# S4D convolution beside a gated unit: preparation queued behind the gated unit's newest VectorE operation, in turns

## The chip, the cores and the metric

The kernel runs on one core of a Trainium2 chip. The metric is the device time of one execution in microseconds (us); of several runs the median is given. The engines are called by the profile's names: PE (TensorE matmuls), PEld (its weight loads), DVE (VectorE), ACT (ScalarE), POOL (GpSimd), SP (SyncE, which here only issues transfers).

## What is computed

One block of a model for 2048 tokens of 448 channels. It adds three terms: the input itself, a long convolution of the normalised input, and a gated unit on the same normalised input.

```python
def ssm(u, log_A_real, A_imag, C_real, C_imag, log_dt, D_skip):
    dt = jnp.exp(log_dt)
    A = -jnp.exp(log_A_real) + 1j * A_imag
    C = (C_real + 1j * C_imag) * dt[:, None]
    P = jnp.exp((A * dt[:, None])[:, :, None] * pos[None, None, :])
    K = 2.0 * jnp.einsum("dn,dnl->dl", C, P).real
    y = jnp.fft.irfft(jnp.fft.rfft(u_t, L2) * jnp.fft.rfft(K, L2), L2)[:, :, :L]
    return y_t + u * D_skip
def glu(x, w_gate, w_up, w_down):
    return (sigmoid(x @ w_gate) * (x @ w_up)) @ w_down
xn = layernorm(A_u)
return A_u + ssm(xn, ...) + glu(xn, ...)
```

Here L is 2048, L2 4096, `u_t` is `u` with channels ahead of tokens, there are 448 channels with 256 states each, and the gated unit has 1792 hidden features.

## The kernel before

**Two streams of work.** The program is written as two generators, `conv()` (L1017) and `glu()` (L727). A loop at the end (L1115) draws from the one whose finished share is smaller; each `yield` gives the planned cost of the work just traced, and the totals stand in L1111. The result is a traced order. From it a scheduler, with a timing estimate of its own, lays down the queue of each engine when the program is built; on the chip each queue runs in that order. Two things bend the order: `hp(HP)` raises the priority of what it encloses, and `tc.issue_after(ins)` keeps the enclosed instructions behind `ins` in the queue of `ins`'s engine. It puts nothing in front of anything.

**The convolution stream.** It normalises the first eight blocks of 128 tokens in two quarters of four and transposes them (`x_transpose`, L191), for the gated unit's first half. It then runs the preparation `prep` (L342), twice, for two halves of the channels (`h` 0 and 1): an exponential by polynomial (`exp`, L300), reciprocals in four pieces (`pieces`, L319), arctangent, sine and hyperbolic tangent on ACT, and phases `U`, `V`, `T` that are split into a high and a low part and stored to memory (L390 to L417). Its `yield`s cut it into portions. Two results, `pl` and `a3`, are turned by TensorE (`turn`, L429, transposes in L436) into the tables `W1` and `GG`. Between portions stand four first stages of the input's transform (`x_spec`, L280). Kernel generation (`kgen`, L458) follows in 56 chunks: POOL forms magnitudes from powers of `W1` (L452), ACT sines of the phases, DVE the products `Et` and `Ft` (L600 to L602), TensorE their sums `ko` (L614). The transforms in `spectra` (L839) come last.

**The gated unit.** It takes the tokens in two halves of 1024, and the 14 feature tiles in groups of three, the last of two. For a feature tile `f` and 512 tokens `t` (here called a unit), `gate` (L693) makes two products of 11 matmuls each (L706), since operands are kept as a high and a low part. ACT forms `th` (L714), DVE `hf` (L717), ACT its high part `hh` (L722), DVE the low part `hl` (L724). At the end of a group come eight products `po` (L817), each added by DVE to `acc` (L822). Weights are loaded by SP (L640, L642) into one buffer, and split by ACT (`wh`, L757) and DVE (`wl`, L761). Gate products, `po` and some others share four PSUM banks (`gu`).

**What orders the work around the change.** All portions of `prep`, and the statistics of the other eight blocks (`x_stats`, L245, L246, and `x_scales`, L248), compete with the gated unit for DVE. The statistics are traced in one piece ahead of the portions, behind the last operation of `x_transpose` (`xls`, L1071). Then, in rounds, one portion of each half is traced behind the third newest `hf` (`hfs`, `LAG`, L1086); a round is planned at 11/3. Transposes of `turn` stay behind the newest gate matmul traced (`glu_mm`, L433). In the traced order the last portion with DVE work lies between the two units of f4, and kernel generation beside the first unit of f5.

In `x_transpose` a quarter has four column blocks. Blocks 0 and 1 lie in one PSUM tile, `tr`, blocks 2 and 3 in tiles of their own, `ko` and `kp`:

```python
two = psc[-1].tile([128, 2, 512], F32, name="tr", bufs=1)
banks = [two[:, 0], two[:, 1]] + [psc[-1].tile([128, 512], F32, name=n, bufs=1) for n in ("ko", "kp")]
```

Each block is transposed (L209), copied by ACT (L218, L221) and subtracted by DVE (L219, L222) before the next block is traced.

Of the kernel before, what the change touches and what calls it, by code (L numbers as in the profile page):

```python
# [11 lines left out]
F32 = mybir.dt.float32  # L12
F32R = mybir.dt.float32r
# [20 lines left out]
WP = 11 / 3  # L34
# [14 lines left out]
LAG = 3  # L49
# [79 lines left out]
def s4d_glu_kernel(ctx, tc, io):  # L129
# [61 lines left out]
    def x_transpose(src, xs, o0):  # L191

        xh, xl, xr = xs
        nb = len(src)
        o = slice(o0, o0 + 128 * nb)

        if nb == 4:
            two = psc[-1].tile([128, 2, 512], F32, name="tr", bufs=1)
            banks = [two[:, 0], two[:, 1]] + [psc[-1].tile([128, 512], F32, name=n, bufs=1) for n in ("ko", "kp")]
        for k in range(4):  # L200
            kp = 128 if k < 3 else 64
            at = k * nb % 4
            if nb == 4:
                ps = banks[k]
            elif at == 0:
                ps = psg.tile([128, 512], F32, name="gu", bufs=4)
            for b in range(nb):
                c = 128 * (at + b)
                nc.tensor.transpose(ps[:kp, c : c + 128], src[b][:, 128 * k : 128 * k + kp], ident)  # L209
            p = ps[:kp, 128 * at : 128 * (at + nb)]  # L210
            if k == 0 and nb == 2:
                continue
            if k == 1 and nb == 2:
                p = ps.rearrange("p (k t) -> p k t", k=2)
                nc.scalar.copy(xh[:, 0:2, o], p)
                v.tensor_tensor(xl[:, 0:2, o], p, xh[:, 0:2, o], ALU.subtract)
            elif k < 3:
                nc.scalar.copy(xh[:, k, o], p)  # L218
                v.tensor_tensor(xl[:, k, o], p, xh[:, k, o], ALU.subtract)  # L219
            else:  # L220
                mv = nc.scalar.copy(xr[0:64, o], p)  # L221
                xls[:] = [v.tensor_tensor(xr[64:128, o], p, xr[0:64, o], ALU.subtract)]  # L222
                act[:] = [mv]

# [468 lines left out]
    def gate(w, xs, to, between=None):  # L693
# [24 lines left out]
        hfs.append(marks[1])  # L718
# [4 lines left out]
        with hp(HP):  # L723
            v.tensor_tensor(hl, hf, hh, ALU.subtract)  # L724
        to.append((hh, hl))

    def glu():  # L727
        stores = []
        for half in range(2):
# [4 lines left out]
            for fs_ in ORDER[half]:  # L734
# [70 lines left out]
                for t in range(2):  # L805
                    acc = accs[2 * half + t]
                    for b in range(4):
# [13 lines left out]
                        with hp(HP):  # L821
                            v.scalar_tensor_tensor(  # L822
                                acc[:, b], po, 0.5, acc[:, b], ALU.mult, ALU.add
                            )
# [192 lines left out]
    def conv():  # L1017
        with tc.tile_pool(name="psk", bufs=1, space=PSUM) as ps_, tc.tile_pool(
# [9 lines left out]
            with tc.tile_pool(name="pst", bufs=1, side="right", reuse_waits="tile") as pst:  # L1028
# [42 lines left out]
                with tc.issue_after(xls[0].ins):  # L1071
                    for b in range(8):
                        x_stats(sm, 8 + b, xes[b // 4][:, b % 4])
                x_scales(sm, 8, 8)

                p01 = pst.tile([CP, 2, 2, 2 * N], F32R, name="p01", tag="xe0")
                for i in range(2):
                    slots[f"P{i}"] = p01[:, i]
                x1ab = pst.tile([128, 2, 2, D], F32, name="x1ab", tag="xe1")
                slots["x1a"], slots["x1b"] = x1ab[:, 0], x1ab[:, 1]  # L1080

                n = 0
# [24 lines left out]
    lasts, glu_mm, sp_mm, glu_on, outs, x1s, hfs, xls = [], [], [], [], [0], [0], [], []  # L1107
# [3 lines left out]
    total = [sum(Y0) + 15 * WP + 8 * WX + 14 + NCK * WK + HOLE + 17 * WS, 2 * (4 + NFT * 14.8) - HELD]  # L1111
# [41 lines left out]
```

## Time and profile before

| | |
|---|---|
| median of 3 runs | 738.23 us (736.59 to 740.59) |
| profiled execution | 739.08 us |
| its span in the trace | 737.3 us |
| TensorE busy | 677.7 us |
| VectorE busy | 565.4 us |

A row of the timeline has the start in the span, the duration (of several in a row, from the first's start to the last's end), engine, line, operation, output and inputs, shapes and count; in brackets the engine's idle time ahead of it and what ended it. Rows of one engine can overlap by some tens of ns, since operations are pipelined. SPq is SP's queue issuing a transfer.

### The profile page before, as it was taken

Reading aid. Unit: us, or ns where it says so; the run is one execution under the profiler, and the core shown is the slowest. Engines: PE = TensorE matmul, PEld = TensorE weight load, DVE = VectorE, ACT = ScalarE, POOL = GpSimd, SP = SyncE. Lnnn points to the kernel's source line nnn. Section 1 sums busy time; section 2 is a strip of 40 time slices with the busy share of each in tenths; the row PEclk is TensorE's granted clock in tenths of the full one; section 3 lists DMA queues with packets and bytes.
Section 4 is the critical chain, followed back from the end, with each engine's and each line's share of the span. In section 5 each row is a group of like instructions: output and inputs, shape, how many; then the busy total and the mean of one; then the engine's idle time right before and its main releaser. Section 6 shows DMA issues by size and latency. Waiting matters only on the chain.

```text
span 737.3 us, 19085 instructions
## 1 busy us (share of the span) xinstructions
PE 677.7 (92%) x7780; PEld 533.9 (72%) x7780; DVE 565.4 (77%) x776; ACT 421.6 (57%) x654; POOL 369.8 (50%) x423
## 2 busy tenths in 40 slices
PE   2896799999998979989999999999999999998994
PEld 2674687887876768655678887888877787775783
DVE  5799997899999888998468969977956555554553
ACT  3534656669679667998467778776643312313310
POOL 2101064987987937865535875877844003241001
PEclk9988999999999999999999999999999999999998
DMA  9935385344413454354953242232269999999756
GB/s 208 227 88 162 80 257 183 99 141 138 157 51 105 155 175 135 109 185 113 289 151 118 76 151 86 77 108 75 75 169 262 261 248 238 230 240 232 182 138 163
DMA packets 93287, 116.76 MB, mean 158 GB/s; under 512 B 12176, under 2 KB 81168, under 8 KB 92944
## 3 DMA queue, kind: packets, MB, share of 16 engines
q1 hardware_dynamic: 83888, 95.08, 47.6%
q10 hardware_dynamic: 6736, 14.57, 6.4%
q0 software_dynamic: 2576, 5.90, 3.4%
q8 instruction: 61, 1.00, 0.6%
q14 instruction: 26, 0.21, 0.1%
HBM read 70.75 MB, written 44.76 MB: 157 GB/s over the span
## 4 chain that ended last, share of the span: by engine, by line
PE 57%; DVE 17%; DMA 9%; POOL 7%; issue 4%; ACT 3%; SPq 3%; ACTq 0%; DVEq 0%; POOLq 0%
PE gu L706 20%; PE po L817 16%; PE sp L899 5%; PE ko L614 5%; PE pv L926 3%; PE tr L538 3%; POOL mf L516 3%; POOL me L516 2%; DVE Ft L602 2%; DVE Et L601 2%; DVE Et L600 1%; DMA sx<-x_d 1%; DMA tb<-in_c_tab_dram 1%; DVE pm L452 1%; PE kp L564 1%
## 5 line engine op out<-in xcount | busy, mean ns | idle before, releaser
L516 POOL TENSOR_TENSOR me<-me,pm 128x32 f32<-128x32 f32 (+1 forms) x168 | 137.0, 815 | 94.0 <-DVE Et L601 85.0
L516 POOL TENSOR_TENSOR mf<-mf,pm 128x64 f32<-128x64 f32 (+1 forms) x112 | 127.2, 1135 | 4.7
L706 PE MATMUL gu<-xh,wh 128*128 128x512 f32 x336 | 102.1, 411 | 3.7 <-ACT xh L218 3.7
L706 PE MATMUL gu<-xh,wl 128*128 128x512 f32 x336 | 96.4, 394 | 0.0
L706 PE MATMUL gu<-xl,wh 128*128 128x512 f32 x336 | 96.2, 391 | 0.0
L817 PE MATMUL po<-dh,hh 128*128 128x448 f32 x224 | 85.5, 382 | 11.3 <-DVE hf L717 7.3
L602 DVE TENSOR_TENSOR Ft<-mf,S 128x1024 f32<-128x1024 f32 x56 | 79.1, 1413 | 17.0 <-PE ko L614 9.3
L601 DVE TENSOR_TENSOR Et<-me,S 128x1024 f32<-128x1024 f32 x56 | 77.9, 1391 | 9.9 <-ACT me L529 8.4
L600 DVE TENSOR_TENSOR Et<-me,S 128x1024 f32<-128x1024 f32 x56 | 80.4, 1438 | 5.8 <-ACT S L549 5.0
L817 PE MATMUL po<-dl,hh 128*128 128x448 f32 x224 | 83.5, 373 | 0.0
L817 PE MATMUL po<-dh,hl 128*128 128x448 f32 x224 | 82.7, 372 | 0.0
L546 ACT ACTIVATE S<-tr 128x1024 f32<-128x1024 f32 x56 | 57.7, 1030 | 42.8 <-PE tr L538 38.5
L614 PEld LDWEIGHTS ko<-Et,Ft 128*32 128x32 f32 x3584 | 54.5, 111 | 35.6 <-DVE Ft L602 15.0
L706 PEld LDWEIGHTS gu<-xh,wh 128*128 128x128 f32 x336 | 62.6, 194 | 23.0 <-ACT xh L218 5.2
L614 PE MATMUL ko<-Et,Ft 128*32 128x64 f32 x3584 | 65.5, 222 | 13.6 <-DVE Ft L602 12.6
L722 ACT CAST hh<-hf 128x512 fp32r<-128x512 f32 x56 | 34.9, 622 | 71.8 <-DVE hf L717 56.3
L706 PEld LDWEIGHTS gu<-xh,wl 128*128 128x128 f32 x336 | 64.1, 191 | 14.8 <-issue 0.7
L706 PEld LDWEIGHTS gu<-xl,wh 128*128 128x128 f32 x336 | 63.1, 188 | 14.1 <-issue 0.7
L822 DVE SCALAR_TENSOR_TENSOR acc<-po,acc 128x448 f32<-128x448 f32 x80 | 48.5, 616 | 22.6 <-PE po L817 22.4
L717 DVE SCALAR_TENSOR_TENSOR hf<-th,gu 128x512 f32<-128x512 f32 x56 | 38.2, 682 | 35.8 <-PE gu L706 31.3
L549 ACT ACTIVATE S<-S,hpi 128x1024 f32<-128x1024 f32 x56 | 65.5, 1169 | 0.0
L714 ACT ACTIVATE th<-gu 128x512 f32<-128x512 f32 x56 | 33.7, 602 | 47.8 <-PE gu L706 47.6
(204 smaller groups left out, 1306.0 us busy)
## 6 DMA issues: line engine op xcount, KB each, us to landing
sk_d<-sk ACTq DMA_DIRECT2D x14, 512.0 KB
sx<-x_d SPq DMA_DIRECT2D x32, 224.0 KB
skl<-sk_d SPq DMA_DIRECT2D x16, 448.0 KB
vp<-v_d SPq DMA_DIRECT2D x16, 448.0 KB
v_d<-vt SPq DMA_DIRECT2D x62, 112.0 KB
wt_d<-wh SPq DMA_DIRECT2D x9, 512.0 KB
wt_d<-wl SPq DMA_DIRECT2D x9, 512.0 KB
wl<-wt_d SPq DMA_DIRECT2D x9, 512.0 KB
```

What stands on the lines that cost most here:

```text
L516: ins = nc.gpsimd.tensor_tensor(m[:, :, w + a : 2 * w : n], m[:, :, a:w:n], par(base + i).unsqueeze(2).to_broadcast([128, 4 * DC, w // n]) ...
L546: nc.scalar.activation(rows(cs), pv, AF.Abs)
L549: sins[:] = [nc.scalar.activation(cs, cs, AF.Sin, scale=-TWO_PI, bias=hpi)]
L600: v.tensor_tensor(Et[:, :, :, 32:64], two(me[:, :, 32:64]), S[:, 1::-1], ALU.mult)
L601: v.tensor_tensor(Et[:, :, :, 0:32], two(me[:, :, 0:32]), S[:, 1:3, :, ::-1], ALU.mult)
L602: fts[:] = [v.tensor_tensor(Ft, two(mf), S[:, 3:5], ALU.mult)]
L614: mm = nc.tensor.matmul(ko[32 * j : 32 * j + 32, sl], Ft[:, cc, DC * h + 4 * q + j], Et[:, cc, DC * h + 4 * q + j], start=(k == 0), stop=( ...
L706: glu_mm[:] = [nc.tensor.matmul(ps, a_, b_, start=(n == 0), stop=(n == len(mm) - 1))]
L717: marks[1] = v.scalar_tensor_tensor(hf, th, 1.0, pgu[1], ALU.add, ALU.mult)
L817: glu_mm[:] = [nc.tensor.matmul(po, a_[:, bs], w_, start=(n == 0), stop=(n == 3 * fc - 1))]
L822: v.scalar_tensor_tensor(acc[:, b], po, 0.5, acc[:, b], ALU.mult, ALU.add)
L899: mm = nc.tensor.matmul(to, tb[:kk, t, 64 * c : 64 * c + 64], rhs, start=True, stop=True, skip_group_check=True,)
```

## The change

Four things are changed. A quarter's sixteen transposes are all traced ahead of its copies. A portion stays behind the newest of `xls`, `hf`, `hl` and `acc`'s addition (`dv`), no longer behind the third newest `hf`. The later statistics become a third generator, four pairs of blocks and then the scales, that takes turns with the two halves. And the planner counts each portion of each generator for itself, at 1.45; before, one round counted 11/3. The tiles that take the place of `xe0` and `xe1` are reserved later, after the statistics that read those.

```diff
-WP = 11 / 3
+WP = 1.45
...
-LAG = 3
...
-        for k in range(4):
+        def turns(ps, k, at):
             kp = 128 if k < 3 else 64
-            at = k * nb % 4
-            if nb == 4:
-                ps = banks[k]
-            elif at == 0:
-                ps = psg.tile([128, 512], F32, name="gu", bufs=4)
             for b in range(nb):
                 c = 128 * (at + b)
                 nc.tensor.transpose(ps[:kp, c : c + 128], src[b][:, 128 * k : 128 * k + kp], ident)
-            p = ps[:kp, 128 * at : 128 * (at + nb)]
+            return ps[:kp, 128 * at : 128 * (at + nb)]
+
+        if nb == 4:
+            parts = [turns(banks[k], k, 0) for k in range(4)]
+        for k in range(4):
+            at = k * nb % 4
+            if nb == 4:
+                p = parts[k]
+            else:
+                if at == 0:
+                    ps = psg.tile([128, 512], F32, name="gu", bufs=4)
+                p = turns(ps, k, at)
...
                 act[:] = [mv]
+                dv[:] = xls
...
-        hfs.append(marks[1])
+        dv[:] = [marks[1]]
...
-            v.tensor_tensor(hl, hf, hh, ALU.subtract)
+            dv[:] = [v.tensor_tensor(hl, hf, hh, ALU.subtract)]
...
-                            v.scalar_tensor_tensor(
+                            dv[:] = [v.scalar_tensor_tensor(
                                 acc[:, b], po, 0.5, acc[:, b], ALU.mult, ALU.add
-                            )
+                            )]
...
-                with tc.issue_after(xls[0].ins):
-                    for b in range(8):
-                        x_stats(sm, 8 + b, xes[b // 4][:, b % 4])
-                x_scales(sm, 8, 8)
-
-                p01 = pst.tile([CP, 2, 2, 2 * N], F32R, name="p01", tag="xe0")
-                for i in range(2):
-                    slots[f"P{i}"] = p01[:, i]
-                x1ab = pst.tile([128, 2, 2, D], F32, name="x1ab", tag="xe1")
-                slots["x1a"], slots["x1b"] = x1ab[:, 0], x1ab[:, 1]
-
+                def later_stats():
+                    for b in (4, 6, 0, 2):
+                        for i in range(2):
+                            x_stats(sm, 8 + b + i, xes[b // 4][:, b % 4 + i])
+                        yield
+                    x_scales(sm, 8, 8)
+                    yield
+
+                preps.append(later_stats())
                 n = 0
                 while preps:
                     for p in list(preps):
                         try:
-                            with tc.issue_after(hfs[max(0, len(hfs) - LAG)].ins), tc.issue_after(act[0].ins):
+                            with tc.issue_after(dv[0].ins), tc.issue_after(act[0].ins):
                                 next(p)
                         except StopIteration:
                             preps.remove(p)
-                    yield WP
+                        yield WP
                     n += 1
                     if n == 2:
                         slots["x1c"] = pst.tile([128, 2, D], F32, name="x1c", tag="raw1")
+                        x1ab = pst.tile([128, 2, 2, D], F32, name="x1ab", tag="xe1")
+                        slots["x1a"], slots["x1b"] = x1ab[:, 0], x1ab[:, 1]
+                    if n == 5:
+                        p01 = pst.tile([CP, 2, 2, 2 * N], F32R, name="p01", tag="xe0")
+                        for i in range(2):
+                            slots[f"P{i}"] = p01[:, i]
...
-    total = [sum(Y0) + 15 * WP + 8 * WX + 14 + NCK * WK + HOLE + 17 * WS, 2 * (4 + NFT * 14.8) - HELD]
+    total = [sum(Y0) + 38 * WP + 8 * WX + 14 + NCK * WK + HOLE + 17 * WS, 2 * (4 + NFT * 14.8) - HELD]
```

More of the change, by code (lines that the diff above doesn't have):

```diff
@@ L1105, in conv @@
             yield from spectra(pf)
-    lasts, glu_mm, sp_mm, glu_on, outs, x1s, hfs, xls = [], [], [], [], [0], [0], [], []
+    lasts, glu_mm, sp_mm, glu_on, outs, x1s, dv, xls = [], [], [], [], [0], [0], [], []
     xq, psc, raws, acl, marks, slots, pqs = list(x_first), [], [], [], [None, None], {}, []
```

## The prediction

> **What bounds the kernel now.** First the page: the busy time of the engines, and the strip of 40 slices (18.4 us each).
>
> ```profile
> PE 677.7 (92%) x7780; PEld 533.9 (72%) x7780; DVE 565.4 (77%) x776; ACT 421.6 (57%) x654; POOL 369.8 (50%) x423
> PE   2896799999998979989999999999999999998994
> DVE  5799997899999888998468969977956555554553
> ```
>
> TensorE is the bound nearly everywhere: 737.3 - 677.7 leaves 59.6 us of idle. What the change touches lies in slices 2 to 6, and there VectorE shows the nines. Next the table of stretches; after the stretch its columns are length, busy time of PE, PEld, DVE, ACT and POOL, granted clock, DMA share, GB/s.
>
> ```profile
> 27.80:111.20 83.40, 68.47 (x335) 53.35 (x335) 82.50 (x143) 46.35 (x80) 17.64 (x11) 0.90 0.57 154
> 92.00:120.00 28.00, 28.00 (x145) 22.68 (x130) 24.26 (x30) 15.36 (x30) 12.52 (x9) 1.00 0.75 222
> 140.00:200.00 60.00, 58.25 (x828) 47.84 (x817) 58.32 (x58) 45.28 (x65) 50.72 (x48) 1.00 0.40 134
> ```
>
> From 27.8 to 111.2, from the gated unit's first VectorE operation to the preparation's last, VectorE works 82.5 of 83.4 us. TensorE idles 83.4 - 68.5 = 14.9 us in that time, but none after 92. From 140 on both are full. The table of waits names TensorE's idle times from 27.8 to 129 (total, times, longest):
>
> ```profile
> PE po L817 <- DVE hf L717: 7.3, 1, 7.3
> PE po L817 <- DVE acc L822: 4.1, 1, 4.1
> PE gu L706 <- ACT xh L218: 3.5, 1, 3.5
> PE tr L538 <- DMA ph<-phv_d: 1.0, 1, 1.0
> ```
>
> The timeline shows how the two long ones arise: preparation stands ahead of the gated unit in VectorE's queue.
>
> ```profile
> 54.24 0.59 ACT L714 ACTIVATE th<-gu 128x512 f32<-128x512 f32 x1
> 61.69 4.99 DVE L321 RECIPROCAL m<-m 112x128 f32<-112x128 f32 x6
> 68.43 0.68 DVE L717 SCALAR_TENSOR_TENSOR hf<-th,gu 128x512 f32<-128x512 f32 x1
> ```
>
> `th` was there at 54.8, `hf` began at 68.4: 13.6 us late.
>
> **The change, part by part.** It computes nothing new; every part moves work.
>
> *The transposes (L209).* Today the second column block of a quarter is transposed only after VectorE has read the first, since both lie in one tile.
>
> ```profile
> 32.26 0.66 PE L209 MATMUL tr<-ident,xn 128*128 128x128 f32 x4
> 35.77 0.57 ACT L218 CAST xh<-tr 128x512 fp32r<-128x512 f32 x1
> 36.39 1.22 PE L706 MATMUL gu<-xh,wh 128*128 128x512 f32 x2 [3.47 <-ACT xh L218]
> 37.84 1.48 PE L706 MATMUL gu<-xh,wl 128*128 128x512 f32 x3
> 39.12 0.63 PE L706 MATMUL gu<-xr,wl 128*128 128x512 f32 x1
> 50.31 0.84 PE L706 MATMUL gu<-xh,wh 128*128 128x512 f32 x3
> 50.99 0.39 PE L706 MATMUL gu<-xr,wh 128*128 128x512 f32 x1
> ```
>
> The late block's copy (35.77) stands on ScalarE behind the preparation's four `Abs` and two `ki`, and TensorE's next gate matmul waits 3.47 us for it. With all sixteen transposes in front, the copies precede the preparation, and this wait goes. After the gap three matmuls take 39.12 - 37.84 = 1.28 us instead of 50.99 - 50.31 = 0.68; at that pace from 36.4 to about 42 another 2.7 us are lost. So TensorE reaches the next units some 6 us earlier. The first quarter gains under 0.5 us likewise.
>
> The Trainium skill, "TensorE: Matmul & The Clock Gate", Part 1, says that the array is throttled to half rate after an idle window of about 3.4 us and released after a window as long of sustained work. The halved pace behind the 3.47 us gap agrees. By that rule gaps that are cut into pieces under 3.4 us would cost no slow stretch at all; that is a rival below.
>
> *The waits behind the newest VectorE operation.* Portions now stay behind the last `hf`, `hl` or `acc` traced, instead of the third newest `hf`. The 7.3 and 4.1 us go with it: `hf` of the third and later units no longer finds 14 us of reciprocals ahead. Slow stretches follow all three gaps. The granted clock of 0.90 over 83.4 us, in the row above, withholds 8.3 us, some of it while TensorE is idle anyway; of the rest 2.7 lie behind the first gap, and I put all three at 5.8. So TensorE could win at most 14.9 + 5.8 = 20.7 us.
>
> But VectorE has no room. What must run before kernel generation (L452) is the same work as now; some of its groups, with the count behind the x, the busy time and the mean in ns, from 27.8 to 111.2, and one group of TensorE (27.8 to 129):
>
> ```profile
> L321 DVE RECIPROCAL pl<-pl 112x128 f32<-112x128 f32 x8 | 6.8, 906 | 0.0
> L321 DVE RECIPROCAL m<-m 112x128 f32<-112x128 f32 x8 | 6.7, 902 | 0.0
> L717 DVE SCALAR_TENSOR_TENSOR hf<-th,gu 128x512 f32<-128x512 f32 x8 | 5.4, 679 | 4.1 <-ACT th L714 4.0
> L724 DVE TENSOR_TENSOR hl<-hf,hh 128x512 fp32r<-128x512 f32 x7 | 4.7, 671 | 0.0
> L245 DVE BATCH_NORM_STATS2 st<-xe 128x6 f32<-128x448 f32 x8 | 4.4, 613 | 0.0
> ```
>
> ```profile
> L278 PE MATMUL tr<-xn,wx 32*64 32x448 f32 x32 | 3.9, 560 | 0.0
> ```
>
> Eight `hf` and seven `hl` run in that time now. Behind the new waits the last portion follows the first `hl` of f4, the ninth of each: one `hf` and two `hl` more, 3 x 0.68 = 2.0 us. The waits also make VectorE idle where it ran ahead before. Between the `hl` of f0 and that of f1 in the second quarter it has only `hf` and `hl`, 0.68 + 0.67, and one of four pairs of statistics, 4.4 / 4 = 1.1, together 2.5 us (the portion traced there is ScalarE's alone). TensorE takes 22 gate matmuls at 0.68 / 3 = 0.227, 5.0, and a first stage (L278, four of them in 3.9), 1.0, together 6.0. So 3.5 us are idle. The round trip `hf`, `hh`, `hl`, which preparation hides today, then shows as it does here:
>
> ```profile
> 114.49 0.69 DVE L724 TENSOR_TENSOR hl<-hf,hh 128x512 fp32r<-128x512 f32 x1 [0.69 <-ACT hh L722]
> ```
>
> I take two of them, 1.4 us, for the two early units in which nothing else is released; there could be none, or one in each of nine units, 6.2. Together 4.9 us idle, with bounds of 3.5 and 9.7. The last portion then ends at 111.2 + 2.0 + 4.9 = 118.1 (116.7 to 122.9).
>
> *Halves and statistics in turns.* The instructions are the same; the first half ends one portion before the second, L420 to L424. Its busy times are 1.9 + 2.5 + 1.3 + 1.2 = 6.9 for both, so 3.4 each:
>
> ```profile
> L421 DVE TENSOR_TENSOR b<-b,m 112x512 f32<-112x512 f32 x2 | 2.5, 1227 | 0.0
> L420 DVE TENSOR_TENSOR a<-a,s 112x512 f32<-112x512 f32 x2 | 1.9, 934 | 0.0
> L422 DVE TENSOR_TENSOR a<-a,b 112x512 f32<-112x512 f32 x2 | 1.3, 680 | 0.0
> L424 DVE TENSOR_SCALAR a<-a,ex 112x256 f32<-112x256 f32 x4 | 1.2, 342 | 0.0
> ```
>
> So the first half is done at 118.1 - 3.4 = 114.7 (113.3 to 119.5). The statistics, 4.4 us and a little, lie between the portions instead of ahead of them; their place costs nothing on an engine that is full, and their scales are used only when the second half's blocks are normalised.
>
> *What is late next.* TensorE's queue holds transposes of the preparation's results (L436), placed between gate matmuls:
>
> ```profile
> 100.08 0.36 PE L436 MATMUL ko<-ident,pl 112*128 112x112 f32 x2
> 113.50 0.36 PE L436 MATMUL ko<-ident,a 112*128 112x112 f32 x2
> 121.31 0.75 DVE L452 SCALAR_TENSOR_TENSOR pm<-W 128x128 f32<-128x128 f32 x1
> 135.52 1.33 DVE L602 TENSOR_TENSOR Ft<-mf,S 128x1024 f32<-128x1024 f32 x1
> 139.43 1.10 PE L614 MATMUL ko<-Et,Ft 128*32 128x64 f32 x64
> ```
>
> Today none waits, because preparation ran ahead. Without its gaps TensorE stands at those of 100.08 up to 20.7 us earlier, at about 80, while the reciprocals and `pl` are spread to later. It waits there instead, and the gate matmuls queued behind it wait with it, though their own inputs are there. It waits again at the pair of 113.50: the input comes at 114.7, plus 0.1 for the release, 1.3 us later than the pair runs today. From there to the first chunk (139.43) TensorE is full but for the 1.0 us of L538, which I take away, since the weight loads ahead of its own loads come sooner. 1.3 - 1.0 = 0.3. VectorE's `Ft` is ready at 136.8 today, 2.6 us ahead of its use, and the powers of L452 stand 121.3 - 111.2 = 10.1 us behind the last portion: that cover takes the 6.9 us by which the portion ends later.
>
> *The queues it moves past.* The portion with `V`, `w`, `T` issues sixteen stores on SP and six subtractions on POOL (L403):
>
> ```profile
> 91.86 0.35 SPq L392 DMA_DIRECT2D phu_d<-p x1
> 108.94 0.77 SPq L392 DMA_DIRECT2D phv_d<-w x1
> 124.62 1.10 SPq L488 DMA_DIRECT2D ph<-phu_d x2
> ```
>
> They move 6.9 us with it, to an end near 117. The loads that read them back begin at 124.6, so about 8 us of cover are left; they cost nothing until that is used up, and then each us counts once.
>
> *The planner's costs.* 15 x 11/3 = 55 becomes 36 portions at 1.45 = 52.2, though the total counts 38 (55.1). That puts the convolution 2.8 units, half a gate, earlier in the trace: no work, at most 5.0 / 2 = 2.5 us of order. I take nothing.
>
> **Sum.** +0.3 us at the first chunk. The bounds are 113.3 and 119.5 in place of 114.7: -1.1 and +5.1. From 140 on it carries through one to one, TensorE being full. The profiled run took 739.08, 1.8 more than its span, and stands 0.85 above the median of 738.23; the shift goes onto the median: 738.5, no change. The 15 us of idle move from `hf` and `acc` to the transposes.
>
> **Rivals.**
>
> Faster: the queue order puts the gated unit's operations first and finds the transposes late enough in TensorE's queue, after two more units. TensorE then keeps half of the 20.7, the 10.1 us that VectorE's powers stand behind the portion being the most that can be made good there: 738.2 - 10.1 = 728. For it: TensorE never idles once VectorE is ahead (92 to 120). Against: VectorE's 82.5 of 83.4 us.
>
> Faster by the clock alone: gaps cut so short that no slow stretch follows, 5.8 us, 732.5. For it: the slow pace comes only behind the three long gaps. Against: two transposes with one late input each make long gaps again. The skill's window, above, is this rival's rule.
>
> Slower: VectorE waits for the round trip in every unit and has more contention with POOL. L413's two operations, with POOL's L403 beside them, take 2.33 us each where others of that shape take 0.68.
>
> ```profile
> L413 DVE TENSOR_TENSOR w<-ki,w 112x512 f32<-112x512 int32 x2 | 4.6, 2333 | 0.0
> ```
>
> The first half ends at the upper bound, 119.5; the pair of 113.50 runs 6.1 us later, a slow stretch of 2.7 follows, and 1.0 goes at L538: +7.8, 746. It decides from the point at which the half ends after 118.1, even without the slow stretch: 118.1 + 0.1 - 113.5 - 1.0 = 3.7.
>
> That the waits bind nothing, the queue being in such an order already, is unlikely: `hf` at 68.4 stands behind portions traced after it. It would leave the transposes' gain, swallowed by VectorE: 738 again.
>
> **How the numbers follow.** Forecast, no change, 0.34; waits that bind nothing, 0.04; faster by order 0.23; faster by the clock 0.08; slower 0.31. Beyond 0.5%, 3.7 us, about what a measurement of this kernel can tell from no change: faster 0.31, same 0.38, slower 0.31. The likeliest case alone spans 734 to 742. The range for 8 in 10 takes in both sides, 728 to 746, and is drawn out by 1 to 3 us, since the schedule behind 140 is laid anew: 727 to 749.
>
> **What would show it.** Right: no wait of po L817 on `hf` and no idle at 33 to 36; waits of ko L436 on VectorE's `pl` and `a` in their place; VectorE with 4 to 6 us more idle before its last L424, which ends near 118; first chunk at 138 to 142. Wrong: no wait at L436, or the first chunk before 135 or after 144, or a difference that arises only after 140.

## The result, and the profile after

The changed kernel took 759.62 us (median of 4 runs, 756.27 to 763.73), the kernel before, beside it, 739.41 (4 runs, 736.59 to 740.72): a ratio of 1.0281, with a 95% interval of 1.022 to 1.0343. The change costs some 20 us. The profiled execution took 760.12 us, its span is 758.3. Line numbers of the kernel after are larger by 5 or 6 from the copies in `x_transpose` on: L218 is now L223, L436 L442, L413 L419, L424 L430, L452 L458, L602 L608, L706 L712.

First the page: busy times, and the granted clock of 40 slices (19.0 us each).

```profile
PE 693.1 (91%) x7780; PEld 543.9 (72%) x7780; DVE 562.4 (74%) x776; ACT 422.5 (56%) x654; POOL 368.0 (49%) x423
PEclk9999998995899999997999899999999999999998
```

TensorE idles 758.3 - 693.1 = 65.2 us, only 5.6 more than before. But it is busy for 15.4 us more with the same instructions: most of the loss is slow clock, and the strip shows where, a 5 at 171 to 190. The table of stretches (columns as before) says it more closely:

```profile
27.80:127.60 99.80, 84.08 (x408) 64.56 (x407) 87.05 (x151) 52.75 (x95) 16.82 (x11) 0.95 0.52 143
92.00:120.00 28.00, 23.03 (x104) 18.05 (x102) 27.16 (x49) 18.43 (x34) 6.23 (x2) 1.00 0.40 122
140.00:200.00 60.00, 48.73 (x590) 38.18 (x589) 50.77 (x51) 47.40 (x66) 51.52 (x54) 0.80 0.34 111
170.00:200.00 30.00, 19.89 (x345) 14.96 (x346) 27.73 (x26) 26.57 (x36) 23.52 (x23) 0.60 0.28 91
```

Preparation now ends at 127.6 in place of 111.2. From 92 to 120, where TensorE was full, it idles 5 us; from 140 to 200, full before at a clock of 1.00, it is busy 48.73 of 60 us at 0.80. The waits of 27 to 129 and then of 129 to 200 (total, times, longest):

```profile
DVE hf L723 <- ACT th L720: 7.4, 2, 4.1
PE gu L712 <- DVE acc L828: 3.4, 1, 3.4
DVE hl L730 <- ACT hh L728: 3.1, 4, 1.3
PE ko L442 <- DVE a L430: 3.0, 2, 2.1
PE gu L712 <- DVE hf L723: 2.8, 2, 2.5
```

```profile
PE ko L620 <- DVE Ft L608: 6.8, 3, 5.0
PE tr L544 <- ACT S L554: 4.2, 4, 2.5
POOL me L497 <- DMA phv_d<-w: 4.0, 1, 4.0
```

The wait of 7.3 us of `po` for `hf` is gone but for 1.2 us in two pieces; shorter ones have come at the gate, and at the transposes (L442, 5.9 us in all their rows). New are waits behind 140, in kernel generation. The timeline shows the stations on the way there:

```profile
116.04 4.59 POOL L409 TENSOR_TENSOR aim<-aim,p 112x512 fp32r<-112x512 f32 x1 [11.63 <-DVE fr L416]
119.43 5.04 DVE L430 TENSOR_SCALAR a<-a,ex 112x256 f32<-112x256 f32 x4
125.59 2.05 DVE L419 TENSOR_TENSOR w<-ki,w 112x512 f32<-112x512 int32 x2
133.11 0.59 SPq L398 DMA_DIRECT2D phv_d<-w  x1
136.79 0.16 POOL L497 MEMSET me<- 128x32 f32 x1 [3.96 <-DMA phv_d<-w]
136.93 0.28 DVE L458 SCALAR_TENSOR_TENSOR pm<-W 128x128 f32<-128x128 f32 x1
137.98 0.73 SPq L494 DMA_DIRECT2D ph<-phu_d  x2
145.67 0.63 PE L544 MATMUL tr<-sel,ph 128*128 128x512 f32 x2
149.89 1.22 DVE L606 TENSOR_TENSOR Et<-me,S 128x1024 f32<-128x1024 f32 x1 [1.64 <-ACT S L555]
152.40 1.64 DVE L608 TENSOR_TENSOR Ft<-mf,S 128x1024 f32<-128x1024 f32 x1
158.08 1.10 PE L620 MATMUL ko<-Et,Ft 128*32 128x64 f32 x64
168.00 0.84 PE L712 MATMUL gu<-xl,wh 128*128 128x512 f32 x3
173.88 1.94 PE L620 MATMUL ko<-Et,Ft 128*32 128x64 f32 x64 [5.04 <-DVE Ft L608]
195.44 1.48 PE L712 MATMUL gu<-xh,wh 128*128 128x512 f32 x3
562.82 1.21 DVE L608 TENSOR_TENSOR Ft<-mf,S 128x1024 f32<-128x1024 f32 x1
```

```profile
540.94 1.22 DVE L602 TENSOR_TENSOR Ft<-mf,S 128x1024 f32<-128x1024 f32 x1
```

The portion with `V`, `w`, `T`, in the middle of preparation's end before (103.2), is now its last: 127.6, and its last store is issued at 133.1. POOL's buffer `me` takes the place of a tile that this store reads, and so waits until 136.8; the powers (L458) run at 136.9 (121.3 before). What the first `Et` waits for in the end is neither, but the sines `S`: the loads that read the phases back (L494) start at 138.0, 13.4 us later than before (124.6), and the transposes they feed (L544) run at 145.7 (128.8 before), behind gate matmuls in TensorE's queue. The first `Ft` ends at 154.0 (136.9 before), the first chunk runs at 158.1, 18.7 us later than before (139.4). TensorE meanwhile went ahead with gate units: before, 264 gate matmuls started ahead of the first chunk, after it is 331. Behind 168.8 it has none left ahead of the next four chunks in its queue: until 195.4 there is no gate product (42 started in that stretch before), only chunks that wait for VectorE, at half pace (64 matmuls in 1.94 us in place of 1.10). The last row, and the single one of the kernel before, are the last chunk's `Ft`: 564.0 and 542.2. Kernel generation ends 21.8 us later, the span 21.0.

An account of what TensorE loses, idle time and busy time withheld by the clock (busy time of each 3 us by one minus the granted clock), closes the picture:

| us lost, from 3 us slices | 0 to 140 | 140 to 220 | 220 to 300 | 300 to 560 | from 560 on | all |
|---|---|---|---|---|---|---|
| before | 35.3 | 3.0 | 11.3 | 5.6 | 13.5 | 68.7 |
| after | 35.0 | 19.9 | 9.4 | 15.8 | 10.0 | 90.1 |

Up to 140, where the change works, nothing is won and nothing lost. The 21 us arise behind it. Chunk by chunk, `Ft` is 17.2 us behind the kernel before at the first chunk, 13.5 at chunk 27, counted from 0, and 23.9 at chunk 36: most of the loss stands at the start of kernel generation, and about 10 us more come between chunks 27 and 36, that is from 348 to 437 us.

### The profile page after: what moved, and what is told of

It is laid out like the page before. It is cut to its first block, busy times and chain, and to the rows that moved or that the text cites. A ratio compares the mean times of both kernels' runs of the same rounds, so it can differ in the third digit from the quotient of the medians.

```text
span 758.3 us, 19091 instructions
## 1 busy us (share of the span) xinstructions
PE 693.1 (91%) x7780; PEld 543.9 (72%) x7780; DVE 562.4 (74%) x776; ACT 422.5 (56%) x654; POOL 368.0 (49%) x423
## 4 chain that ended last, share of the span: by engine, by line
PE 55%; DVE 21%; ACT 9%; DMA 5%; issue 5%; POOL 2%; SPq 1%; ACTq 1%; DVEq 0%; POOLq 0%
PE gu L712 21%; PE po L823 13%; PE sp L905 6%; PE ko L620 5%; PE pv L932 3%; DVE Ft L608 3%; DVE Et L606 3%; PE tr L544 3%; DVE Et L607 2%; DMA acc<-in_A_u_dram 2%; DVE hl L730 2%; DVE pm L458 1%; ACT S L555 1%; PE kp L570 1%; DVE hf L723 1%
## 5 line engine op out<-in xcount | busy, mean ns | idle before, releaser
L522 POOL TENSOR_TENSOR me<-me,pm 128x32 f32<-128x32 f32 (+1 forms) x168 | 141.7, 844 | 112.5 <-DVE Et L607 101.6
L522 POOL TENSOR_TENSOR mf<-mf,pm 128x64 f32<-128x64 f32 (+1 forms) x112 | 123.1, 1099 | 4.9
L712 PE MATMUL gu<-xh,wh 128*128 128x512 f32 x336 | 104.4, 416 | 8.6 <-DVE acc L828 3.4
L712 PE MATMUL gu<-xh,wl 128*128 128x512 f32 x336 | 98.3, 401 | 0.0
L712 PE MATMUL gu<-xl,wh 128*128 128x512 f32 x336 | 96.8, 395 | 0.0
L620 PEld LDWEIGHTS ko<-Et,Ft 128*32 128x32 f32 x3584 | 57.6, 116 | 41.1 <-DVE Ft L608 19.4
L620 PE MATMUL ko<-Et,Ft 128*32 128x64 f32 x3584 | 68.3, 230 | 20.2 <-DVE Ft L608 18.2
L712 PEld LDWEIGHTS gu<-xh,wh 128*128 128x128 f32 x336 | 63.1, 196 | 31.7 <-issue 5.8
L608 DVE TENSOR_TENSOR Ft<-mf,S 128x1024 f32<-128x1024 f32 x56 | 79.4, 1417 | 4.1 <-POOL mf L522 3.1
L712 PEld LDWEIGHTS gu<-xh,wl 128*128 128x128 f32 x336 | 65.4, 195 | 14.7
L712 PEld LDWEIGHTS gu<-xl,wh 128*128 128x128 f32 x336 | 64.3, 192 | 13.7
L723 DVE SCALAR_TENSOR_TENSOR hf<-th,gu 128x512 f32<-128x512 f32 x56 | 38.1, 681 | 42.6 <-PE gu L712 27.8
L730 DVE TENSOR_TENSOR hl<-hf,hh 128x512 fp32r<-128x512 f32 x56 | 50.4, 900 | 19.3 <-ACT hh L728 19.3
```

Source lines behind the costliest of these rows:

```text
L522: ins = nc.gpsimd.tensor_tensor(m[:, :, w + a : 2 * w : n], m[:, :, a:w:n], par(base + i).unsqueeze(2).to_broadcast([128, 4 * DC, w // n]) ...
L608: fts[:] = [v.tensor_tensor(Ft, two(mf), S[:, 3:5], ALU.mult)]
L620: mm = nc.tensor.matmul(ko[32 * j : 32 * j + 32, sl], Ft[:, cc, DC * h + 4 * q + j], Et[:, cc, DC * h + 4 * q + j], start=(k == 0), stop=( ...
L712: glu_mm[:] = [nc.tensor.matmul(ps, a_, b_, start=(n == 0), stop=(n == len(mm) - 1))]
L723: marks[1] = v.scalar_tensor_tensor(hf, th, 1.0, pgu[1], ALU.add, ALU.mult)
L730: dv[:] = [v.tensor_tensor(hl, hf, hh, ALU.subtract)]
```

## The experiments

Two theories stood at the start. **W**: the new waits make preparation late, and the powers with it. **P**: the planner's new counts and the turns lay the order of the whole program anew. The readings of all runs first, but for b_probe, which adds work of its own; "last" is where preparation's last VectorE operation ends (`a` or `T`), then the ends of the first and the last `Ft`, in the profiled run of each.

| kernel | against before, 95% | last | first Ft | last Ft |
|---|---|---|---|---|
| before | 1 | 111.2 | 136.9 | 542.2 |
| after | 1.0281 [1.022, 1.0343] | 127.6 | 154.0 | 564.0 |
| b_pins: the waits alone | 1.0089 [1.0057, 1.0122] | 120.1 | 146.0 | 549.8 |
| b_turns: turns and counts alone | 1.021 [1.0167, 1.0253] | 118.7 | 144.4 | 555.0 |
| b_tr: the transposes alone | 1.0045 [1.0017, 1.0074] | 113.6 | 140.9 | 545.5 |
| a_lag3: after without the waits | 1.0205 [1.014, 1.0269] | 117.4 | 144.7 | 558.4 |
| b_cost: the counts alone | 1.0161 [1.0121, 1.0202] | 110.3 | 141.1 | 553.8 |
| b_halves: halves in turns alone | 1.0026 [0.9999, 1.0053] | 112.9 | 136.6 | 542.7 |
| b_stats: statistics in turns alone | 1.0042 [1.0014, 1.0071] | 110.2 | 139.9 | 546.8 |
| a_wp1: after, portions traced earlier | 1.021 [1.0157, 1.0263] | 121.7 | 146.6 | 555.4 |
| a_mend: after, counts that add up | 1.0181 [1.0158, 1.0204] | 127.5 | 148.6 | 555.5 |
| b_late: counts the other way | 1.0174 [1.0129, 1.0218] | 117.6 | 146.5 | 556.8 |
| b_cost_st: b_cost, a store moved | 1.0112 [1.0081, 1.0143] | 110.3 | 141.6 | 549.2 |
| b_pins_old: b_pins, late portions free | 1.0069 [1.0043, 1.0095] | 117.1 | 144.2 | 549.3 |
| a_less: after without statistics | 1.0251 [1.0213, 1.029] | 125.2 | 150.6 | 560.0 |
| b_cost_half: half of b_cost's shift | 0.9978 [0.9951, 1.0004] | 110.3 | 140.8 | 539.9 |
| b_st: the store moved alone | 0.9981 [0.9955, 1.0007] | 113.0 | 138.9 | 543.2 |
| b_cost_full: b_cost, 128 rows | 1.0119 [1.0062, 1.0176] | 111.4 | 140.4 | 549.4 |
| b_best | 0.9959 [0.9933, 0.9986] | 110.2 | 139.6 | 536.0 |

Two things hold in every row. The first `Ft` ends 21 to 31 us behind the last of preparation. And the span ends 193 to 200 us behind the last `Ft` (737.3 - 542.2 = 195.1, 758.3 - 564.0 = 194.3): to within some 7 us the time is where kernel generation ends.

### The parts, one at a time

**b_pins**

```diff
-with tc.issue_after(hfs[max(0, len(hfs) - LAG)].ins), tc.issue_after(act[0].ins):
+with tc.issue_after(dv[0].ins), tc.issue_after(act[0].ins):
```

> The kernel before with one part of the change alone: portions behind the newest VectorE operation of the gated unit; statistics, rounds, planner's costs and transposes as before. Theory W (the waits make the preparation late, so kernel generation starts late): about 753 to 760, the powers near 135 instead of 121. Theory P (the planner's new costs and the turns move the order): 735 to 742, the powers near 121.

**b_turns**

```diff
-WP = 11 / 3
+WP = 1.45
...
+preps.append(later_stats())
...
-total = [sum(Y0) + 15 * WP ...
+total = [sum(Y0) + 38 * WP ...
```

> The kernel before with the turns alone: halves and later statistics in turns, each portion planned at 1.45 and 38 of them in the total, still behind the third newest hf, transposes as before. Theory W: 735 to 743, powers within 5 us of 121. Theory P: 750 to 760, powers near 135.

**b_tr**

```diff
+if nb == 4:
+    parts = [turns(banks[k], k, 0) for k in range(4)]
```

> The kernel before with the transposes of a quarter alone queued as one. Both theories: 733 to 740; the wait of 3.5 us on the copy is smaller or gone, and VectorE, which is full until 111, takes most of it back. A third theory, that the transposes spoil the early order, would give over 745.

**a_lag3**

```diff
-with tc.issue_after(dv[0].ins), tc.issue_after(act[0].ins):
+with tc.issue_after(hfs[max(0, len(hfs) - 3)].ins), tc.issue_after(act[0].ins):
```

> The changed kernel with the waits alone undone: portions behind the third newest hf again, turns, costs and transposes as changed. Theory W: 733 to 743, powers near 121. Theory P: 752 to 760, powers near 135.

The waits alone cost 6.7 us (746.02 against 739.34), the turns with their counts 16.5 (755.89), the transposes 2.9 (742.20). Taking the waits out of after leaves 757.61. Two of the four fit theory P, b_turns and a_lag3; b_pins lies between the two theories, and b_tr just above the range that both gave it. So W falls as the main cause, though it is not nothing, and P explains more. No part gains, the transposes neither.

### Which of the turns

**b_cost**

```diff
-WP = 11 / 3
+WP = 3.48
...
-total = [sum(Y0) + 15 * WP ...
+total = [sum(Y0) + 38 * 1.45 ...
```

> The kernel before with nothing but the planner's numbers of after: 15 rounds at 3.48 (52.2 in all) where the total counts 55.1. Theory P (the planner's numbers carry most of what the turns cost, since kernel generation is then traced 2.8 units earlier against the gated unit): 1.012 to 1.022, with the second jump of 6 to 9 us at chunks 27 to 36 that the turns alone showed. Theory T (the turns themselves cost it, by a later preparation on VectorE): 0.997 to 1.005, no jump.

**b_halves**

```diff
-    yield WP
+        yield WP / 2
```

> The kernel before with the two halves in turns only: each half's portion is counted for itself at 11/6, so the total stays 55; the statistics stay ahead of all portions. Theory T, if the halves are what costs: 1.010 to 1.020, first Ft 4 us or more later than before. Theory P, and theory T with the statistics as what costs: 0.996 to 1.006.

**b_stats**

```diff
-with tc.issue_after(xls[0].ins):
-    for b in range(8):
-        x_stats(sm, 8 + b, xes[b // 4][:, b % 4])
-x_scales(sm, 8, 8)
...
+preps.append(later_stats())
...
```

> The kernel before with the later statistics as a third generator only, in the same rounds with the same count of 55, and the tiles that follow them reserved later. Theory T, if the statistics between the portions are what costs: 1.010 to 1.020, first Ft 4 us or more later. Theory P, and theory T with the halves as what costs: 0.996 to 1.006.

**a_mend**

```diff
-WP = 1.45
+WP = 55 / 36
...
-total = [sum(Y0) + 38 * WP ...
+total = [sum(Y0) + 36 * WP ...
```

> The kernel after with nothing but counts that add up: 36 portions at 55/36 and a total with 36, so that kernel generation stands in the traced order where it stood before. Theory P (the 2.8 units missing from the count cost about 12 us of the 20): 1.006 to 1.018, what waits, transposes and turns cost by themselves. Its rival (in after the late portion with V, w, T decides, the count adds nothing to it): 1.022 to 1.034, first Ft still at 150 or later.

b_cost changes two numbers and no instruction, and takes 750.28 us against 738.83: 11.5 us of the turns' 16.5. Halves and statistics cost 2.5 and 2.3 us by the medians (741.38, 741.14), the halves within what can be told from nothing (the interval reaches down to 0.9999). Mending the count in after gives back 7.5 us (752.12 against 759.62), and leaves 1.0181, the upper edge of what theory P expected. The count is the largest single part that was measured.

### Is it the size of the shift?

**b_late**

```diff
-WP = 11 / 3
+WP = 3.855
...
-total = [sum(Y0) + 15 * WP ...
+total = [sum(Y0) + 55 ...
```

> The kernel before with 15 rounds at 3.855, 57.8 in all, where the total still counts 55: kernel generation is traced 2.8 units later against the gated unit, as far as b_cost had it earlier. If earlier is what costs (TensorE's gate work then stands behind kernel generation and weights behind phase loads): 0.990 to 1.003. If any move from the old place costs, the old order being a fortunate one: 1.008 to 1.02.

**b_cost_half**

```diff
-WP = 11 / 3
+WP = 3.573
...
-total = [sum(Y0) + 15 * WP ...
+total = [sum(Y0) + 55 ...
```

> The kernel before with 15 rounds at 3.573, 53.6 in all, where the total still counts 55: half of the shift of b_cost, kernel generation 1.4 units earlier in the traced order. If the shift costs by its size: 1.006 to 1.011. If each new order is a draw of its own, the old one being a fortunate one: anything from 1.002 to 1.02 with a place of first loss of its own, not half of b_cost's in the same places.

Kernel generation 2.8 units later costs 1.0174, 2.8 earlier 1.0161, 1.4 earlier nothing (0.9978). It isn't a price by the unit, though 0.9978 lies below both expectations for b_cost_half: the theory of draws, too, had expected a loss. The three look as if each new order were a draw and the old one a good one; three orders don't show that. The two that lose do so in different places: b_late by a late preparation (117.6, the first `Ft` 9.6 us late), b_cost not (110.3). b_cost_half and b_cost stay within 7 us of each other up to chunk 27, counted from 0 (`Ft` 4 and 2 us behind the kernel before); at chunk 30 they stand at -2 and +12, at chunk 36 at -3 and +15. So what separates them lies between 300 and 400. The kernel after, a_lag3 and a_mend, too, fall back between chunks 27 and 36, by 10, 11 and 6 us.

### What costs in b_cost: a store in SP's queue, and the clock

Around 180 in b_cost, a chain over four engines:

```profile
172.24 2.12 POOL L787 TENSOR_TENSOR dl<-rd,dh 128x448 fp32r<-128x448 f32 x1
174.39 0.34 SPq L778 DMA_DIRECT2D dt_d<-dl  x1
174.77 1.67 SPq L642 DMA_DIRECT2D wraw<-in_B_w_up_dram  x2
178.17 1.05 ACT L757 CAST wh<-wraw 128x1024 fp32r<-128x1024 f32 x1 [6.59 <-DMA wraw<-in_B_w_up_dram]
179.25 1.23 DVE L761 TENSOR_TENSOR wl<-wraw,wh 128x1024 fp32r<-128x1024 f32 x1 [4.33 <-ACT wh L757]
182.26 1.93 PE L614 MATMUL ko<-Et,Ft 128*32 128x64 f32 x64 [7.54 <-DVE Ft L602]
```

POOL makes `dl` late, behind its magnitudes. SP's queue holds dl's store, and the up weights' loads behind it; ACT waits for the weights, VectorE for ACT, and with it the `Ft` that stands behind `wl`, and TensorE waits 7.54 us.

**b_cost_st**

```diff
-stores.extend(kept((dh, dl), dt_d, f))
+high, low = kept((dh, dl), dt_d, f)
+stores.append(high)
+nc.gpsimd.dma_start(low[1], low[0])
```

> b_cost with one store moved: the low part of the down weights (dl) is stored by POOL's own queue behind the subtraction that makes it, no longer by SP's, where it holds up the loads of gate and up weights behind it (SP issued it at 174.4 in b_cost, 6 us behind the row ahead of it). If that queue makes TensorE's 7.5 us wait for Ft at 182: the wait falls under 2 us, ACT's wait for wraw under 1 us, and the time by 4 to 8 us, 1.005 to 1.011. If not: the wait stays above 5 us and 1.013 to 1.02.

```profile
178.43 1.10 PE L614 MATMUL ko<-Et,Ft 128*32 128x64 f32 x64 [3.17 <-DVE Ft L602]
```

ACT's wait for the weights is gone, TensorE's falls to 3.17 us, between the two expectations, and the time to 747.17, 3 us won, at the edge of what was expected. So the chain is shown; the 3.17 us that are left have another cause, since VectorE works without a pause ahead of them.

**b_st** is the same edit to the kernel before.

> The kernel before with dl's store on POOL's queue behind the subtraction that makes it, in place of SP's. If SP's queue costs nothing in the old order (its weights are loaded 10 us ahead): 0.998 to 1.004. If the store holds up loads there too: 0.988 to 0.997.

It changes nothing that can be measured there (0.9981): in the old order the weights are loaded long before.

Then the stretch from 300 to 400. In b_cost the clock is low in it (columns as above), and TensorE's longest wait there is 1.0 us:

```profile
310.00:320.00 10.00, 7.74 (x118) 3.59 (x106) 9.44 (x9) 10.00 (x18) 7.63 (x8) 0.80 0.44 131
320.00:330.00 10.00, 10.00 (x92) 7.47 (x91) 6.17 (x10) 6.04 (x12) 6.55 (x11) 0.69 0.65 178
340.00:350.00 10.00, 9.51 (x127) 4.39 (x125) 6.14 (x8) 4.37 (x10) 3.88 (x4) 0.84 0.58 207
350.00:360.00 10.00, 10.00 (x64) 6.83 (x60) 3.03 (x6) 5.12 (x9) 0.00 (x0) 0.65 0.36 84
360.00:370.00 10.00, 10.00 (x91) 4.60 (x79) 5.31 (x7) 5.69 (x10) 4.42 (x9) 0.69 0.56 173
```

The products of busy time and withheld clock sum to 13 us. Ahead of the first slow stretch stand first stages of the later blocks, on 32 rows and 64 columns of the array, and no gate product between 308.5 and 320.4:

```profile
310.67 0.97 PE L278 MATMUL gu<-xt,wx 32*64 32x448 f32 x4
312.10 0.97 PE L278 MATMUL gu<-xt,wx 32*64 32x448 f32 x4 [0.46 <-DVE xl L216]
313.34 0.97 PE L278 MATMUL gu<-xt,wx 32*64 32x448 f32 x4
```

**b_probe** measures such matmuls by themselves, behind the kernel's end, in a single run. Its edit is shortened here, with comments added.

```diff
+dense(60)                                  # 128x512, 128*128
+for i in range(80): nc.tensor.matmul(...)  # 64x448, 32*64
+dense(60)
+for i in range(800): nc.tensor.matmul(...) # 32x64, 128*32
+dense(60)
+for i in range(120): nc.tensor.transpose(...)
+dense(60)
```

> The kernel before with seven stretches of matmuls on constants behind its last use of TensorE, no idle between them: 60 of 128x512 with the whole array, 80 of 64x448 with 32 rows and 64 columns, the 60 again, 800 of 32x64 with 32 columns, the 60, 120 transposes, the 60. Theory C (small tiles and transposes don't hold the granted clock, so that stretches without gate products are followed by half pace though TensorE is never idle for 1 us): the clock falls to 0.5 within the small stretches and in the first 3 us or so of the 60 that follow them, which then take 2 us or more longer than a stretch at full clock. Its rival (only idle lowers the clock): 1.0 from the first stretch's start-up on to the end.

Seven of its 4 us stretches: the 32-row matmuls from 741.8 to 795.9, gate-like ones behind them, the 32-column matmuls from 811.1 to 853.3, the transposes from 867.1 to 880.1.

```profile
740.00:744.00 4.00, 4.00 (x21) 2.08 (x21) 0.00 (x0) 0.00 (x0) 0.00 (x0) 1.00 0.00 0
744.00:748.00 4.00, 4.00 (x24) 1.41 (x22) 0.00 (x0) 0.00 (x0) 0.00 (x0) 0.96 0.00 0
748.00:752.00 4.00, 4.00 (x14) 1.42 (x12) 0.00 (x0) 0.00 (x0) 0.00 (x0) 0.50 0.00 0
796.00:800.00 4.00, 4.00 (x12) 3.22 (x13) 0.00 (x0) 0.00 (x0) 0.00 (x0) 0.64 0.00 0
800.00:804.00 4.00, 4.00 (x20) 3.30 (x19) 0.00 (x0) 0.00 (x0) 0.00 (x0) 1.00 0.00 0
844.00:848.00 4.00, 1.99 (x128) 1.84 (x128) 0.00 (x0) 0.00 (x0) 0.00 (x0) 1.00 0.01 4
872.00:876.00 4.00, 4.00 (x39) 4.00 (x38) 0.00 (x0) 0.00 (x0) 0.00 (x0) 1.00 0.00 0
```

The 32-row matmuls keep TensorE busy without a gap, and from about 748 on they run at half clock until 796; the whole-array matmuls behind them have it back after some 3 us. The 32-column ones, with pauses of half the time, and the transposes stay at 1.00. So theory C holds for 32 rows by 64 columns, and is wrong for the other two. Whether the rows count or the share of the array that a tile fills (32 x 64 against 128 x 32) was not tried.

**b_cost_full** fills the weights of the 32-row matmuls of that stretch up to 128 rows with zeros, which adds one fill and four small loads in the first 40 us.

```diff
-x_first_stage(pss[g][:, :D], xns, g)
+for i in range(2):
+    nc.tensor.matmul(pss[g][64 * i : 64 * i + 64, :D], wz[:, g], xns[i], start=True, stop=True)
```

> b_cost with the 32 first-stage matmuls of the later blocks (L278, in the gated unit's last group of the first half) over all 128 rows of the array in place of 32, their weights filled up with zeros; the result is the same, and the order of TensorE's queue stays, but for these matmuls themselves. Theory C (matmuls on 32 rows let the granted clock fall as idle does; in b_cost they stand together without gate products between them, and the slow clock of 300 to 400 is the 12 us by which b_cost is slower): the 13.3 us that the slow clock costs there fall below 5, the matmuls themselves cost up to 4 us more, and the time is 739 to 746, 1.000 to 1.010. Its rival (the slow clock follows the idle times): 13 us as before, 750 to 756, 1.015 to 1.024.

```profile
310.00:320.00 10.00, 7.75 (x110) 3.51 (x98) 9.50 (x9) 10.00 (x18) 7.63 (x8) 0.83 0.44 129
320.00:330.00 10.00, 9.12 (x100) 6.21 (x98) 8.53 (x11) 8.87 (x15) 7.57 (x11) 1.00 0.60 178
350.00:360.00 10.00, 10.00 (x113) 6.16 (x113) 7.67 (x11) 7.10 (x12) 1.25 (x3) 1.00 0.61 182
```

The slow stretches behind 320 are gone, the one just ahead stays (0.83 in place of 0.80), the 13 us of withheld clock fall to 1.5, and four matmuls take 0.97 us on 128 rows as on 32. The clock went as theory C said. The time didn't: 749.23 us, 1.0119, between the two expectations; by the spans (751.2 and 746.3) 4.9 us are won, and b_cost's interval is overlapped. So the clock is at most a part of b_cost's 12 us. The account of lost time, in slices of 2 us, says where the rest went: 10.4 us less are lost from 300 to 400, 3.5 more from 400 to 560, and what TensorE works, counted at full clock, is 3.4 us more, a sum that varies by as much from run to run.

### How far the late preparation reaches

**b_pins_old**

```diff
-with tc.issue_after(dv[0].ins), ...
+with tc.issue_after((dv[0] if n < 10 else hfs[max(0, len(hfs) - LAG)]).ins), ...
```

> b_pins with the new waits for the first ten rounds of portions only; from the portion with U on, with V, w, T and the last ones behind it, a portion stays behind the third newest hf as before. Theory L (the new waits cost what they delay the stores of V, w, T, on which powers and kernel generation stand): V, w, T end before 115 in place of 120.1, first Ft at 138 to 142 in place of 146, 0.998 to 1.005. Its rival (the waits cost by the order that they leave from 140 on): 1.006 to 1.012.

**a_wp1**

```diff
-WP = 1.45
+WP = 1.0
```

> The kernel after with each portion counted at 1.0 in place of 1.45: preparation is traced about 16 units, three gates, earlier against the gated unit, and with it the operations that its portions are kept behind. Theory L (after loses its time because the portion with V, w, T and its stores come 24 us late, powers and kernel generation follow, and the gate work done meanwhile is missing as filler at 170 to 200): that portion ends before 118 in place of 127.6, the first Ft before 147 in place of 154, the clock of 170 to 200 back above 0.85, and a time of 740 to 750 (1.002 to 1.014). Its rival (the loss is made by the order from 140 on, whatever preparation does): 1.018 or more with an early first Ft.

**a_less** leaves out the statistics of blocks 8 to 15, which are then normalised with those of the first blocks.

```diff
-for i in range(2):
-    x_stats(sm, 8 + b + i, xes[b // 4][:, b % 4 + i])
 yield
```

> The kernel after without the later statistics' L251 and L252 (blocks 8 to 15 are then normalised with the first blocks' statistics): 4.4 us and a little less work for VectorE ahead of the last portion, all else as traced in after. Theory V (VectorE's own work sets when preparation and then kernel generation come): last L419 and first Ft 4 to 6 us earlier than in after (127.6 and 154.0), and the time 3 to 6 us below after, 1.020 to 1.024. Its rival (the round trips between VectorE and ScalarE, with gated units between them, set it, VectorE has room): both ends within 2 us of after's, 1.026 to 1.031.

b_pins_old moves the last portion by 3 us, the first `Ft` by 2, too little to decide; its 1.0069 lies in the range of theory L's rival. a_wp1 brings the first `Ft` from 154.0 to 146.6, as expected, though its portion with `V`, `w`, `T` ends at 121.7 and not before 118; the clock of 170 to 200 rises from 0.60 to 0.80, short of 0.85, and the time is 754.76, 1.021, where theory L alone has 1.014 at most: the rival's forecast holds, 1.018 or more with an early first `Ft`. Its TensorE loses 19.3 us between 140 and 220, after's 19.9, with such a stretch of its own: no gate product from 159.3 to 179.2. So a first `Ft` 7 us earlier doesn't do away with the stretch without gate work; the order of TensorE's queue has a part in it. In a_less 5.7 us less of VectorE's work (L251 4.6, L252 1.1) bring the last portion 2.4 us and the first `Ft` 3.4 us earlier, and the time to 1.0251, between the two expectations: VectorE's own work sets the late start in part only. So the late start is one part of the loss, and the order behind it another.

### A version that beats both

**b_best** joins b_cost_half, b_st and the 128-row first stages.

> The kernel before with the three edits that cost nothing or seemed to gain: kernel generation 1.4 units earlier (15 rounds at 3.573 where the total counts 55), dl's store on POOL's queue, and the later blocks' first stages over all 128 rows. If their small gains are real and add: 0.990 to 0.997. If each new traced order is a draw of its own: anywhere from 0.995 to 1.015, with the last chunk's end moved by as much.

It took 735.21 us (12 runs) against 737.40: 0.9959 [0.9933, 0.9986], 0.4% faster than the kernel before. That lies in both expected ranges, so it doesn't tell gains that add from a lucky order. It contains no part of the change but a smaller shift of the count.

## Why the prediction was wrong

It said 738.5 us, 727 to 749, no change; 759.62 is above the range. The sum had the first chunk 0.3 us later, 5.1 at most; it came 18.7 later, and what followed was not carried through one to one. Two of the prediction's own signs of being wrong came true: a first chunk after 144, and a difference that arises only after 140. Step by step:

- **What bounds the kernel.** Right for the kernel before. "From 140 on it carries through one to one, TensorE being full" is the step that failed most: after, TensorE is busy 48.73 of 60 us there at 0.80, and 17 of the 21 us arise between 140 and 220. The full engine of before is not a property of the stage but of the gate work that stands beside the chunks in the queue: after, the chunks come later while the gate goes on, and from 168.8 to 195.4 none is left beside them.
- **The transposes.** The sixteen did go together, but ACT's copy of block 1 stays behind the four `Abs` (33.8 us), the wait is 1.5 us in place of none, and by itself the edit costs 0.45%.
- **The waits.** Right that the 7.3 us go. VectorE's idle time was mis-sized: from 27.8 to 127.6 it idles 99.80 - 87.05 = 12.75 us, 11.9 more than before, where I put 4.9 and at most 9.7; the waits of `hf` for `th` alone are 7.4. It works 4.6 us more where I put 2.0; the four scalings of L430 take 5.04 us with POOL at work beside them, mostly on L409, where four took 1.2.
- **The queues it moves past.** "They move 6.9 us with it, to an end near 117", with "about 8 us of cover": the portion with `V`, `w`, `T` moved 24.4 us, the last store came at 133.1, and the cover was used up: the loads moved by 13.4 us. The sum followed the transposes of the results (L436, now L442) to the first chunk; the way that came last ran over these loads, the transposes that they feed (L544) and the gate matmuls queued ahead of those. I took it that portions keep their order; the one with the longest chain of hops between VectorE and ScalarE fell to the end.
- **The planner's costs.** "No work, at most 5.0 / 2 = 2.5 us of order. I take nothing." In the kernel before, these two numbers alone cost 11.5 us, the largest part measured. I priced the shift by its size; b_cost_half and b_late show that it has no price by size.
- **The rivals.** Slower had its sign right, but its price (746) is far below, and its place, waits at L442 of 5.9 us, is not where most was lost. Neither faster case has any support. The one by the clock fails as a mechanism too: from 27 to 126 TensorE's waits are cut to 3.4 us and less, yet from 125.7 to 130.9 it runs at a clock of 0.50, behind 6.9 us in which it was busy for 1.75 and never idle for more than 2.1 at a time.

What stays open: of the parts' ratios (1.6, 0.9, 0.45, 0.4 and 0.3 per cent, 3.6 in sum) after shows 2.8, so they don't simply add, and which us of after belongs to which can't be said. Nor does one stretch explain every run: a_lag3 loses only 9.2 us between 140 and 220 and takes 757.61. Why some 10 us more are lost between 300 and 560 in after isn't settled either, beyond the likeness to b_cost; why the scheduler's order turns out so for one count and not for another stays open too.

## What to carry to other kernels

Where two streams share an engine, look for the work that one keeps at hand for the other's waits: what runs while one stream is late is missing beside it later. A planner's count that no longer adds up is a change of the program, to be measured by itself before the edit that brought it. Of a moved portion, follow the one with the most hops between engines up to its last store, and the buffers that wait for that store.

## What the runs showed of the hardware

- The granted clock falls without idle: 32-row matmuls back to back ran at 0.50 for 48 us (b_probe), and it fell to 0.50 in after behind gaps of 2.1 us at most with little work between them (busy 1.75 of 6.9 us, then 0.50 from 125.7 to 130.9). The Trainium skill, "TensorE: Matmul & The Clock Gate", Part 1, ties the throttle to idle windows of about 3.4 us. The runs agree on the time scale, some 3 to 5 us to recover (796 to 799 in b_probe, 125.7 to 130.8 in after), but show that being busy isn't enough.
- Transposes held the clock. The Trainium skill, "TensorE: Matmul & The Clock Gate", Part 4, says that transposes don't count as busy in that way. In b_probe 13 us of transposes of FP32 tiles, which the profile lists as matmuls with `ident`, stayed at 1.00 behind whole-array matmuls; whether they would also raise a low clock no run here shows.
- Filling 32-row weights up to 128 rows didn't lengthen the matmuls: 0.97 us for four either way.
- VectorE's L430 took 1.22 to 1.36 us each while POOL worked on tensors beside it (L409 and L793), and 0.34 with POOL idle (before). One L409, begun 3.4 us ahead of them, took 4.59 us; the two that ran beside L430 alone took 1.3.
